# GpSimd scales the exponent half of VectorE's exponentials; the last VectorE step becomes a 16-bit integer sum

## The chip, the core and the metric

The kernel runs on one core of a Trainium2 chip. A core has five engines that work side by side and are held together by semaphores: TensorE (PE in the profile; its weight loads are PEld), VectorE (DVE), ScalarE (ACT), GpSimd (POOL) and SyncE (SP), which only issues DMAs. SBUF is the on-chip memory, PSUM the memory into which TensorE accumulates. The metric is the time of the program on the device in microseconds (us); lower is better.

## What is computed

Two layers; each is an attention block followed by a token-mixing MLP, on x of [1, 2048, 640], with the same weights in both layers.

```python
def _A_ref(x, wqkv, wo):                      # 32 heads of 20
    q, k, v = ...(x @ wqkv)                   # B,H,S,Dh each
    scores = jnp.einsum("bhqd,bhkd->bhqk", q, k) * (Dh ** -0.5)
    p = _softmax(scores, axis=-1)
    o = jnp.einsum("bhqk,bhkd->bhqd", p, v)
    return (heads side by side) @ wo
def _B_ref(x, w1, b1, w2, b2):                # mixes along the tokens
    h = _layernorm(x, axis=-1)
    u = _gelu(jnp.einsum("bsd,sf->bdf", h, w1) + b1)
    return transposed(jnp.einsum("bdf,fs->bds", u, w2) + b2)
x = A_x
x = x + _A_ref(_layernorm(x), A_wqkv, A_wo);  x = x + _B_ref(_layernorm(x), ...)
x = x + _A_ref(_layernorm(x), A_wqkv, A_wo);  x = x + _B_ref(_layernorm(x), ...)
```

What matters here is the softmax: 32 heads of 2048 by 2048 exponentials in each layer, 134 million in a layer.

## The kernel before, in words

**Tiling.** Scores are made transposed, keys on the 128 partitions, 512 queries in the free dimension, for 4 heads at a time (a group). One such 128 x 512 block of one head is called a chunk here. A layer has 4 query blocks x 8 groups x 16 key tiles = 512 units (`NU`, line 252) of 4 chunks (`NH`), 2048 chunks; the two layers have 4096. A unit's scores (lines 642 to 647) go to PSUM tiles `S` of three or two chunks; ScalarE takes the exponential of a whole `S` tile into a bf16 tile `P` (`emit_exp`, L715); TensorE multiplies `P` with the values and adds into the PSUM tile `acc` (`emit_PV`, L1268), where a column of ones gives the softmax's denominator as well.

**Exponentials on VectorE.** Some chunks are taken from ScalarE. TensorE writes such a chunk's scores to the PSUM tile `Dt` (`ve_admit`, lines 507 to 554), and VectorE makes exp of it from integer operations. The scores come scaled so that the float is a fixed-point base-2 exponent with 16 fraction bits. Two chunks form a pair `p` with slots 0 and 1:

- `first` (L544): add the exponent's bias, clamp at zero, write as int32 into `ew`; one instruction for each chunk, reading PSUM. The upper 16 bits of each word are the whole part of the exponent, the lower 16 the fraction; both are read as 16-bit elements at a step of two.
- the shift (L604): `ey` = the fraction, scaled and moved, as f16. It runs on GpSimd where `ve_shift` (lines 607 to 625) could place it, else on VectorE (`shifted`).
- `squared` (L574): `ey` = `ey` * `ey`, a dense f16 product over the pair.
- `mantissa` (L578): `et` = (`ey` + constant) * fraction, over the pair, written as f32: the mantissa's part of the result's bits.
- `expo` (L587): `Pd` = whole * 128 + `et`, over the pair, written as int16 into the bits of the bf16 tile `Pd`. `Pd` then goes to L1268 like a `P`.

**What sets the order.** The instruction streams of VectorE, ScalarE, GpSimd and TensorE are written out by a planner that runs when the kernel is built. It keeps a clock for each engine (`pem`, `dvm`, `acm`) and one for the SBUF port that VectorE and GpSimd share (`port`). Work on VectorE is a list of `Proc` objects, each a row of steps (planned cost, function, wait, and a fourth element if the step needs the shared port: `locks()`, line 294). `pump` (line 332) takes the step that can start first, by rank among those within 0.06 us: normalisation of a finished `acc` 0, evacuation of other PSUM tiles 1, `first` 2, layer norm 3, the pair's other steps 4. A locking step starts no earlier than `port["pool"]` (line 302), the planned end of GpSimd's last shift.

`ve_shift` is called from `Proc.step` (lines 306 and 307) when a step that does not lock and costs at least `POOL_HOST` = 0.45 us is about to run: that step is the **host** of a GpSimd instruction, which is issued beside it and held by a semaphore until the VectorE instruction before the host has ended (`after_vector`). Hosts are the instructions that read PSUM or have one SBUF input: L544, the transposes L752 and L776, the evacuations L364, L366, L1018, L1023, L1071 and L1105 and the statistics L828 and L831.

`ve_admit` gives VectorE another chunk whenever `Dt` is free, the planned backlog of VectorE is at most `VE_BACKLOG` = 7 us and, for a new pair, no more than two pairs are queued; so the planner keeps VectorE full, and what VectorE takes ScalarE does not have to do (`take_acts`, line 484). VectorE's pairs exist only after the first weights and keys have been made (`late`, `feed_ended`) and until the units run out. TensorE's gaps are filled with products of zeros (`zero_wave`, L704), which keep it busy and whose results are not used.

Of the kernel before, what the change touches and what calls it, by code (L numbers as in the profile page):

```python
# [12 lines left out]
BF16 = mybir.dt.bfloat16  # L13
F32 = mybir.dt.float32
I32 = mybir.dt.int32
I16 = mybir.dt.int16
# [3 lines left out]
ALU = mybir.AluOpType  # L20
# [38 lines left out]
POOL_EY = 0.58  # L59
POOL_NEXT = 0.144  # L60
POOL_TO_DVE = 0.1
POOL_LATE = 0.3
POOL_HOST = 0.45
POOL_DMA = 0.9

HOLD = 3
# [11 lines left out]
def kernel(  # L78
# [12 lines left out]
    nc = tc.nc  # L91
# [11 lines left out]
    def after_vector(inst):  # L103
        earlier = next(i for i in reversed(nc.cur_bb.bb.instructions) if i.engine == nc.vector.engine)
        tc.add_manual_dep(inst.ins, earlier.name,
                          mybir.DependencyInfo(mybir.DependencyClass.Sync, mybir.DependencyReason.DATA), reason="port")
# [113 lines left out]
    def attention(st, x_in_ap, x_mid, uacc_l, feed, feed_stack):  # L220
# [14 lines left out]
        late = {}  # L235

        def open_late():
            def pool(name, bufs):
                late[name] = p1.enter_context(tc.tile_pool(name=f"{name}{layer}", bufs=bufs, reuse_waits="tile"))
            pool("xsp", 3 if x_in_ap.dtype == F32 else 2)  # L240
            pool("w1sp", 2)
            pool("ustg", 2)
            pool("atp", NG + 4)
            pool("vew", 3)
            pool("vet", 1)
            pool("vey", 2)
            pool("vep", 3)
        T2 = ntmp.tile([128, 16, 32], BF16, name="T2")
        nc.gpsimd.memset(T2[:], 0.0)
        h2_tiles, tt_state, attnT_tiles = {}, {}, {}  # L250
# [9 lines left out]
        port = dict(pool=0.0, t=0.0)  # L260
# [25 lines left out]
        class Proc:  # L286
# [17 lines left out]
            def step(self):  # L304
                at = self.start()
                if self.eng is dvm and not self.locks() and self.steps[0][0] >= POOL_HOST:
                    ve_shift(at)
                cost, fn, wait = self.steps.popleft()[:3]
                end = at + cost
                self.eng["t"] = end - self.eng["over"]  # L310
                self.ready = end + self.eng["next"] + wait
                fn(end)
                if not self.steps:
                    self.eng["procs"].remove(self)
                    if self.after is not None:
                        self.after(end)
# [190 lines left out]
        def ve_admit(t):  # L507
            now = pem["t"] - WAVE
            if (not late or early[0] or cursor[0] >= NCH or Dbank.free > now + 0.02 or
                    backlog(now) > CFG["VE_BACKLOG"]):  # L510
                return
            p, slot = ve_state["pair"], ve_state["slot"]
            if slot == 0:
                if len(ve_procs) > 2:
                    return
                done = backlog(now) + 2 * 1.2 + 4.0 + CFG["VE_MARGIN"]
                n = max(cursor[0] // NH + max(CFG["VE_LEAST"], math.ceil(done / 1.8)), ve_state["unit"] + 1)
                if n >= NU:
                    n = max(cursor[0] // NH + math.ceil((done - CFG["VE_MARGIN"]) / 1.8), ve_state["unit"] + 1)
                if n >= NU and Dbank not in banks:  # L520
                    banks.append(Dbank)
                if n >= NU or not unit_ok(units[n], now - 0.1):
                    return
                ve_state["unit"] = n
            n = ve_state["unit"]
            js = {c[1] for c in tiles[t]}
            free = [j for j in range(NH) if (n, j) not in on_dve]
            c = (n, next((j for j in free if j not in js), free[0]))
            clash = c[1] in js
            on_dve.add(c)  # L530
            loc[c] = (p, slot)
            ve_users.setdefault(p, []).append(c)
            ve_shifted.setdefault(p, [])
            Dt = Dbank.alloc()
            s_matmul(Dt[:, :], *c)
            at = pe_wave("S", cells=0.25) if clash else now
            Dbank.free = 1e9
            if slot == 0:
                ve_w[p] = late["vew"].tile([128, 2, 512], I32, name="ew")
            w = ve_w[p]  # L540

            def first(end):
                Dbank.free = end + DVE_TO_PE
                nc.vector.tensor_scalar(out=w[:, slot, :], in0=Dt[:, :], scalar1=127.0 * FIX,  # L544
                                        scalar2=0.0, op0=ALU.add, op1=ALU.max)

            def firsted(end):
                pieces.append((p, slot, w, end))
                if slot == 1:
                    ve_enqueue(p, 2, end + DVE_NEXT)  # L550
            submit(Proc(2, [(0.69, first, 0.0)], at + PE_TO_DVE, after=firsted))
            ve_state["slot"] = 1 - slot
            if slot == 1:
                ve_state["pair"] = p + 1

        def ve_enqueue(p, k, ready):
            w = ve_w.pop(p)
            wh = w[:, 0:k, :].rearrange("p a b -> p (a b)").bitcast(I16).rearrange("p (c two) -> p c two", two=2)
            frac = wh[:, :, 0].bitcast(U16)
            whole = wh[:, :, 1]  # L560
            vet, vep = late["vet"], late["vep"]
            box = {}

            def shifted(end):
                todo = [x for x in range(k) if x not in ve_shifted[p]]
                c0, c1 = 512 * todo[0], 512 * (todo[-1] + 1)
                for x in list(pieces):
                    if x[0] == p:
                        pieces.remove(x)
                shift(nc.vector, ve_y_of(p)[:, c0:c1], frac[:, c0:c1])  # L570

            def squared(end):
                y = ve_y_of(p)[:, 0:512 * k]
                nc.vector.tensor_tensor(out=y, in0=y, in1=y, op=ALU.mult)  # L574

            def mantissa(end):
                box["t"] = vet.tile([128, 1024], F32, name="et")
                nc.vector.scalar_tensor_tensor(out=box["t"][:, 0:512 * k], in0=ve_y.pop(p)[:, 0:512 * k],  # L578
                                               scalar=MANT_C * MANT_K ** 2, in1=frac, op0=ALU.add, op1=ALU.mult)

            def expo(end):
                Pd = vep.tile([128, 2, 512], BF16, name="Pd")
                ve_P[p] = Pd
                bits = Pd[:, 0:k, :].rearrange("p a b -> p (a b)").bitcast(I16)
                ve_ready[p] = end + DVE_TO_PE
                ve_procs.popleft()
                nc.vector.scalar_tensor_tensor(out=bits, in0=whole, scalar=128.0, in1=box["t"][:, 0:512 * k],  # L587
                                               op0=ALU.mult, op1=ALU.add)
            steps = [(0.15 + 0.27 * (k - len(ve_shifted[p])), shifted, 0.0, True)] if len(ve_shifted[p]) < k else []
            steps += [(0.69, squared, 0.0, True), (1.22, mantissa, 0.0, True), (1.22, expo, 0.0, True)]  # L590
            proc = Proc(4, steps, ready, allow=lambda me: ve_procs[0] is me and (len(me.steps) > 1 or p - 3 not in ve_users))
            proc.pair, proc.ready = p, max([ready] + ve_shifted_at.get(p, []))
            ve_procs.append(proc)
            dvm["procs"].append(proc)

        ve_y, ve_shifted, ve_shifted_at = {}, {}, {}

# [6 lines left out]
            return engine.tensor_scalar(out=out_ap, in0=in_ap, scalar1=MANT_K / FIX, scalar2=-MANT_K * MANT_S,  # L604
                                        op0=ALU.mult, op1=ALU.add)

        def ve_shift(at):
            if not pieces or pieces[0][3] + POOL_NEXT > at + POOL_LATE or port["t"] > at + POOL_LATE:
                return
            if pieces[0][0] - 2 in ve_y:  # L610
                return
            p, slot, w, end = pieces.popleft()
            half = w[:, slot, :].bitcast(I16).rearrange("p (c two) -> p c two", two=2)[:, :, 0].bitcast(U16)
            inst = shift(nc.gpsimd, ve_y_of(p)[:, 512 * slot:512 * (slot + 1)], half)
            after_vector(inst)
            done = max(at + POOL_NEXT, end + POOL_NEXT, port["t"]) + POOL_EY
            port["pool"] = port["t"] = done
            ve_shifted[p].append(slot)
            ve_shifted_at.setdefault(p, []).append(done + POOL_TO_DVE)
            for proc in ve_procs:  # L620
                if proc.pair == p:
                    cost, fn, wait, lock = proc.steps.popleft()
                    if cost > 0.5:
                        proc.steps.appendleft((cost - 0.27, fn, wait, lock))
                    proc.ready = max(proc.ready, done + POOL_TO_DVE)
# [739 lines left out]
        t = 0  # L1365
# [455 lines left out]
```

## Time and profile before

| | us |
|---|---|
| median of 3 runs (1764.66 to 1764.97) | 1764.69 |
| the profiled execution: its own time | 1764.66 |
| its span, first to last instruction | 1762.8 |
| busy: PE / ACT / DVE / POOL | 1686.9 / 1676.8 / 1536.8 / 379.6 |
| granted TensorE clock | 1.0 |

The profile is of one execution. A line of its groups names a source line, the engine, the operation, what is written and read by the program's names, the shapes, the count, then the busy time, the mean of one in ns, and the idle time of that engine before them with what ended it. The windows view gives each engine's busy time, and its number of instructions, in a stretch of the span. A line of the timeline gives start, duration, the instruction, and the idle time before it.

### The profile page before, as it was taken

Reading aid. Unit: us, or ns where it says so; the run is one execution under the profiler, and the core shown is the slowest. Engines: PE = TensorE matmul, PEld = TensorE weight load, DVE = VectorE, ACT = ScalarE, POOL = GpSimd, SP = SyncE. Lnnn points to the kernel's source line nnn. Section 1 sums busy time; section 2 is a strip of 40 time slices with the busy share of each in tenths; the row PEclk is TensorE's granted clock in tenths of the full one; section 3 lists DMA queues with packets and bytes.
Section 4 is the critical chain, followed back from the end, with each engine's and each line's share of the span. In section 5 each row is a group of like instructions: output and inputs, shape, how many; then the busy total and the mean of one; then the engine's idle time right before and its main releaser. Section 6 shows DMA issues by size and latency. Waiting matters only on the chain. (4 is left out here: it accounts for less than half of the span.)

```text
span 1762.8 us, 42985 instructions
## 1 busy us (share of the span) xinstructions
PE 1686.9 (96%) x18044; PEld 669.7 (38%) x18044; DVE 1536.8 (87%) x2356; ACT 1676.8 (95%) x1510; POOL 379.6 (22%) x597
## 2 busy tenths in 40 slices
PE   9999999999999999999999999999999999999999
PEld 3333333333333344444444433333333333444455
DVE  7479999999999999999543469999999999999973
ACT  8999999999999999999779999999999999999970
POOL 2112222222232223221000011122222332322200
PEclk9999999999999999999999999999999999999999
DMA  3200000010122110123322100001001220101345
GB/s 116 39 2 1 1 2 2 16 32 2 35 63 72 38 36 14 40 76 118 113 79 74 56 20 1 1 2 39 24 2 61 68 80 14 62 2 52 102 125 178
DMA packets 103010, 81.85 MB, mean 46 GB/s; under 512 B 50976, under 2 KB 87456, under 8 KB 102816
## 3 DMA queue, kind: packets, MB, share of 16 engines
q1 hardware_dynamic: 97280, 71.22, 13.7%
q0 software_dynamic: 5536, 7.88, 1.4%
q8 instruction: 141, 2.31, 0.6%
q14 instruction: 53, 0.43, 0.1%
HBM read 55.48 MB, written 23.59 MB: 45 GB/s over the span
## 5 line engine op out<-in xcount | busy, mean ns | idle before, releaser
L715 ACT ACTIVATE P<-S 128x1024 bf16<-128x1024 f32 (+1 forms) x1442 | 1629.2, 1387 | 13.0 <-PE S L645 12.7
L645 PE MATMUL S<-QTq,KT 32*128 32x512 bf16 (+1 forms) x4488 | 577.5, 337 | 65.6 <-ACT P L715 46.7
L604 POOL TENSOR_SCALAR ey<-ew 128x512 f16<-128x512 uint16 x494 | 305.0, 617 | 1019.7 <-DVE et L578 415.9
L645 PEld LDWEIGHTS <-KT 32*128 32x128 bf16 x5136 | 232.4, 91 | 534.4 <-issue 507.0
L1268 PE MATMUL acc<-P,Vaug 128*32 128x512 bf16 (+1 forms) x4472 | 362.4, 343 | 0.3 <-ACT P L715 0.3
L544 DVE TENSOR_SCALAR ew<-Dt 128x512 int32<-128x512 f32 x496 | 338.3, 682 | 17.2 <-PE Dt L645 11.1
L704 PE MATMUL acc<-zr,zw 128*32 128x512 bf16 x4408 | 343.8, 383 | 1.2 <-POOL zr L151 1.2
L587 DVE SCALAR_TENSOR_TENSOR Pd<-ew,et 128x1024 int16<-128x1024 int16 x248 | 311.9, 1258 | 1.2
L578 DVE SCALAR_TENSOR_TENSOR et<-ey,ew 128x1024 f32<-128x1024 f16 x248 | 302.4, 1219 | 2.4
L645 PE MATMUL Dt<-QTq,KT 32*128 32x512 bf16 (+1 forms) x648 | 190.8, 332 | 0.0
L574 DVE TENSOR_TENSOR ey<-ey 128x1024 f16<-128x1024 f16 x248 | 174.2, 702 | 0.4
L1268 PEld LDWEIGHTS <-Vaug 128*32 128x32 bf16 x5120 | 103.0, 94 | 169.9 <-issue 158.9
L704 PEld LDWEIGHTS <-zw 128*32 128x32 bf16 x4620 | 116.9, 96 | 99.5 <-issue 54.7
L845 POOL TENSOR_TENSOR rstd<-veps,mhalf 128x1 f32<-128x1 f32 x60 | 49.0, 817 | 252.3 <-DVE veps L843 197.3
L1268 PE MATMUL acc<-Pd,Vaug 128*32 128x512 bf16 (+1 forms) x648 | 97.5, 334 | 0.2 <-DVE Pd L587 0.2
L1119 PE MATMUL misc<-hh,wq_pad 128*128 128x512 bf16 x300 | 87.3, 383 | 0.0
L1010 PEld LDWEIGHTS <-w1st 128*128 128x128 bf16 x672 | 52.1, 97 | 58.6 <-issue 46.5
L1119 PE MATMUL misc<-hh,wk_pad 128*128 128x512 bf16 x250 | 73.2, 383 | 0.0
L752 DVE STREAM_TRANSPOSE T<-acc 128x512 f32<-128x512 f32 (+1 forms) x81 | 56.3, 695 | 19.3 <-PE acc L1268 19.0
L1059 PE MATMUL misc<-wo_pad,attnT 128*128 128x320 bf16 x384 | 72.8, 302 | 0.3 <-DVE x1s L1071 0.2
L1010 PE MATMUL misc<-x1last,w1st 128*128 128x320 bf16 x384 | 72.1, 302 | 0.0
L364 DVE CAST KT<-misc 128x512 bf16<-128x512 f32 x50 | 34.3, 685 | 20.8 <-PE misc L1119 20.7
(143 smaller groups left out, 1083.8 us busy)
## 6 DMA issues: line engine op xcount, KB each, us to landing
w2s<-in_B_w_dram SPq DMA_DIRECT2D x16, 768.0 KB
uacc<-ustg POOLq DMA_DIRECT2D x24, 320.0 KB, 2.7
x1in<-xd SPq DMA_DIRECT2D x24, 320.0 KB
w1st<-in_B_w_dram SPq DMA_DIRECT2D x24, 256.0 KB
xd<-x2s SPq DMA_DIRECT2D x16, 320.0 KB
xin<-xd SPq DMA_DIRECT2D x16, 320.0 KB
w1st<-in_B_w_dram SPq DMA_DIRECT2D x24, 192.0 KB
xd<-x1s SPq DMA_DIRECT2D x12, 320.0 KB
```

Of the source, the lines that this page charges most:

```text
L544: nc.vector.tensor_scalar(out=w[:, slot, :], in0=Dt[:, :], scalar1=127.0 * FIX, scalar2=0.0, op0=ALU.add, op1=ALU.max)
L574: nc.vector.tensor_tensor(out=y, in0=y, in1=y, op=ALU.mult)
L578: nc.vector.scalar_tensor_tensor(out=box["t"][:, 0:512 * k], in0=ve_y.pop(p)[:, 0:512 * k], scalar=MANT_C * MANT_K ** 2, in1=frac, op0=ALU ...
L587: nc.vector.scalar_tensor_tensor(out=bits, in0=whole, scalar=128.0, in1=box["t"][:, 0:512 * k], op0=ALU.mult, op1=ALU.add)
L604: return engine.tensor_scalar(out=out_ap, in0=in_ap, scalar1=MANT_K / FIX, scalar2=-MANT_K * MANT_S, op0=ALU.mult, op1=ALU.add)
L645: pe(nc.tensor.matmul(out_ap[:, c0:c0 + w], lhsT=KT[32 * j:32 * j + 32, g, kt * 128:(kt + 1) * 128], rhs=get_QT(st, qb)[32 * j:32 * j + 32 ...
L704: pe(nc.tensor.matmul(bank[32 * j:32 * j + 32, 0:w], lhsT=zw[:], rhs=zr[:, :, 0:64].to_broadcast([128, w // 64, 64]), start=start, stop=st ...
L715: nc.scalar.activation(out=P[:, 0:ncs, :].rearrange("p a b -> p (a b)"), in_=St[:, 0:ncs, :].rearrange("p a b -> p (a b)"), func=ACT.Exp, ...
L1010: pe(nc.tensor.matmul(t[:, 0:w], lhsT=w1_of[(p, ft)][:, sti, :], rhs=rows_in[sti][:, c0:c1], start=(sti == 0), stop=(sti == n_in - 1)))
L1059: pe(nc.tensor.matmul(t[:, 0:w], lhsT=attnT[g][:, ttl * 128:(ttl + 1) * 128], rhs=wo_pad[:, g, c0:c1], start=(g == 0), stop=(g == NG - 1)))
L1119: pe(nc.tensor.matmul(t[:, :], lhsT=wpad[:, dt_, g, :], rhs=hT[:, dt_, tb * 512:(tb + 1) * 512], start=(dt_ == 0), stop=(dt_ == NDT - 1)))
L1268: pe(nc.tensor.matmul(acc[32 * j:32 * j + 32, a0:a0 + w], lhsT=Vaug[:, (kt * H + hh_) * VW:(kt * H + hh_) * VW + 32], rhs=P[:, slot, c0:c0 ...
```

## The change

`ve_base` is new. Where a host finds no shift to place, it may place a **base** instead: GpSimd multiplies the whole part of one chunk (512 elements at a step of two, int16) by 128 into that chunk's half of the result tile `Pd`, as int16. `expo` then differs by what was placed: both halves based, one dense `tensor_tensor` sum of `Pd` and `et` in place; one half based, two instructions of 512 elements, a sum for that half and the old operation for the other; none, the old instruction. `et` is int16 in place of f32, so that the sum has 16-bit operands only. `Pd` has four buffers in place of three, and is allocated by whichever of `ve_base` and `expo` comes first. The planner's cost of `expo` is 1.22, 1.03 or 0.69 us for no, one or two bases.

```diff
--- before.py
+++ after.py
@@ -61,6 +61,9 @@
 POOL_TO_DVE = 0.1
 POOL_LATE = 0.3
 POOL_HOST = 0.45
+POOL_BASE_HOST = 0.45
+VEP_BUFS = 4
+VE_ADD = (1.22, 1.03, 0.69)
 POOL_DMA = 0.9
 
 HOLD = 3
@@ -244,7 +247,7 @@
             pool("vew", 3)
             pool("vet", 1)
             pool("vey", 2)
-            pool("vep", 3)
+            pool("vep", VEP_BUFS)
         T2 = ntmp.tile([128, 16, 32], BF16, name="T2")
         nc.gpsimd.memset(T2[:], 0.0)
         h2_tiles, tt_state, attnT_tiles = {}, {}, {}
@@ -304,7 +307,7 @@
             def step(self):
                 at = self.start()
                 if self.eng is dvm and not self.locks() and self.steps[0][0] >= POOL_HOST:
-                    ve_shift(at)
+                    ve_shift(at, self.steps[0][0])
                 cost, fn, wait = self.steps.popleft()[:3]
                 end = at + cost
                 self.eng["t"] = end - self.eng["over"]
@@ -546,6 +549,7 @@
 
             def firsted(end):
                 pieces.append((p, slot, w, end))
+                bases.append((p, slot, w, end))
                 if slot == 1:
                     ve_enqueue(p, 2, end + DVE_NEXT)
             submit(Proc(2, [(0.69, first, 0.0)], at + PE_TO_DVE, after=firsted))
@@ -558,7 +562,6 @@
             wh = w[:, 0:k, :].rearrange("p a b -> p (a b)").bitcast(I16).rearrange("p (c two) -> p c two", two=2)
             frac = wh[:, :, 0].bitcast(U16)
             whole = wh[:, :, 1]
-            vet, vep = late["vet"], late["vep"]
             box = {}
 
             def shifted(end):
@@ -574,24 +577,62 @@
                 nc.vector.tensor_tensor(out=y, in0=y, in1=y, op=ALU.mult)
 
             def mantissa(end):
-                box["t"] = vet.tile([128, 1024], F32, name="et")
+                box["t"] = late["vet"].tile([128, 1024], I16, name="et")
                 nc.vector.scalar_tensor_tensor(out=box["t"][:, 0:512 * k], in0=ve_y.pop(p)[:, 0:512 * k],
                                                scalar=MANT_C * MANT_K ** 2, in1=frac, op0=ALU.add, op1=ALU.mult)
 
             def expo(end):
-                Pd = vep.tile([128, 2, 512], BF16, name="Pd")
+                Pd = ve_result(p)
                 ve_P[p] = Pd
-                bits = Pd[:, 0:k, :].rearrange("p a b -> p (a b)").bitcast(I16)
                 ve_ready[p] = end + DVE_TO_PE
                 ve_procs.popleft()
-                nc.vector.scalar_tensor_tensor(out=bits, in0=whole, scalar=128.0, in1=box["t"][:, 0:512 * k],
-                                               op0=ALU.mult, op1=ALU.add)
+                for x in [x for x in bases if x[0] == p]:
+                    bases.remove(x)
+                based = ve_based.pop(p, [])
+                parts = [range(k)] if len(based) in (0, k) else [[x] for x in range(k)]
+                for part in parts:
+                    lo, hi = 512 * part[0], 512 * (part[-1] + 1)
+                    bits = Pd[:, 0:k, :].rearrange("p a b -> p (a b)").bitcast(I16)[:, lo:hi]
+                    t = box["t"][:, lo:hi]
+                    if part[0] in based:
+                        nc.vector.tensor_tensor(out=bits, in0=bits, in1=t, op=ALU.add)
+                    else:
+                        nc.vector.scalar_tensor_tensor(out=bits, in0=whole[:, lo:hi], scalar=128.0, in1=t,
+                                                       op0=ALU.mult, op1=ALU.add)
             steps = [(0.15 + 0.27 * (k - len(ve_shifted[p])), shifted, 0.0, True)] if len(ve_shifted[p]) < k else []
-            steps += [(0.69, squared, 0.0, True), (1.22, mantissa, 0.0, True), (1.22, expo, 0.0, True)]
-            proc = Proc(4, steps, ready, allow=lambda me: ve_procs[0] is me and (len(me.steps) > 1 or p - 3 not in ve_users))
+            cost = VE_ADD[min(2, len(ve_based.get(p, [])) + 2 - k)]
+            steps += [(0.69, squared, 0.0, True), (1.22, mantissa, 0.0, True), (cost, expo, 0.0, True)]
+            proc = Proc(4, steps, ready, allow=lambda me: ve_procs[0] is me and
+                        (len(me.steps) > 1 or p in ve_results or p - VEP_BUFS not in ve_users))
             proc.pair, proc.ready = p, max([ready] + ve_shifted_at.get(p, []))
             ve_procs.append(proc)
             dvm["procs"].append(proc)
+
+        ve_results, ve_based, bases = {}, {}, deque()
+
+        def ve_result(p):
+            if p not in ve_results:
+                ve_results[p] = late["vep"].tile([128, 2, 512], BF16, name="Pd")
+            return ve_results[p]
+
+        def ve_base(at):
+            for x in bases:
+                p, slot, w, end = x
+                if end + POOL_NEXT > at + POOL_LATE or port["t"] > at + POOL_LATE:
+                    return
+                if p not in ve_results and (p - VEP_BUFS in ve_users or p - 1 not in ve_results and p > 0):
+                    return
+                bases.remove(x)
+                bits = ve_result(p)[:, slot, :].bitcast(I16)
+                whole = w[:, slot, :].bitcast(I16).rearrange("p (c two) -> p c two", two=2)[:, :, 1]
+                after_vector(nc.gpsimd.tensor_scalar(out=bits, in0=whole, scalar1=128.0, scalar2=0.0, op0=ALU.mult, op1=ALU.add))
+                port["pool"] = port["t"] = max(at + POOL_NEXT, end + POOL_NEXT, port["t"]) + POOL_EY
+                ve_based.setdefault(p, []).append(slot)
+                for proc in ve_procs:
+                    if proc.pair == p:
+                        cost, fn, wait, lock = proc.steps.pop()
+                        proc.steps.append((VE_ADD[len(ve_based[p])], fn, wait, lock))
+                return
 
         ve_y, ve_shifted, ve_shifted_at = {}, {}, {}
 
@@ -604,10 +645,11 @@
             return engine.tensor_scalar(out=out_ap, in0=in_ap, scalar1=MANT_K / FIX, scalar2=-MANT_K * MANT_S,
                                         op0=ALU.mult, op1=ALU.add)
 
-        def ve_shift(at):
-            if not pieces or pieces[0][3] + POOL_NEXT > at + POOL_LATE or port["t"] > at + POOL_LATE:
-                return
-            if pieces[0][0] - 2 in ve_y:
+        def ve_shift(at, self_cost):
+            if (not pieces or pieces[0][3] + POOL_NEXT > at + POOL_LATE or port["t"] > at + POOL_LATE or
+                    pieces[0][0] - 2 in ve_y):
+                if self_cost >= POOL_BASE_HOST:
+                    ve_base(at)
                 return
             p, slot, w, end = pieces.popleft()
             half = w[:, slot, :].bitcast(I16).rearrange("p (c two) -> p c two", two=2)[:, :, 0].bitcast(U16)
```

## The prediction

> **What bounds the kernel now.** I read the busy time by stretch first, since shares over the whole span mix stages. This is the windows view, on the two stretches from the first to the last `ew` instruction of each layer, where VectorE's pairs exist (columns: the stretch, its length, then busy time and instructions of PE, PEld, DVE, ACT, POOL):
>
> ```profile
> 109.40:811.20 701.80, 672.81 (x7694) 253.68 (x7693) 687.14 (x973) 701.50 (x622) 182.28 (x286) 1.00 0.10 30
> 1037.70:1689.70 652.00, 624.19 (x7162) 240.87 (x7160) 638.86 (x924) 652.00 (x578) 166.96 (x258) 1.00 0.12 35
> ```
>
> ACT is busy for 701.5 of 701.8 and all of 652.0 us: it sets the length of both. DVE is 98% busy (1326.0 of 1353.8 us, 27.8 idle), so it has nothing to give. PE looks as busy, but the page's L704 group, products of zeros, is 343.8 us of it. POOL is idle three quarters of the time. Next, the costliest groups (page, part 5):
>
> ```profile
> L715 ACT ACTIVATE P<-S 128x1024 bf16<-128x1024 f32 (+1 forms) x1442 | 1629.2, 1387 | 13.0 <-PE S L645 12.7
> ...
> L604 POOL TENSOR_SCALAR ey<-ew 128x512 f16<-128x512 uint16 x494 | 305.0, 617 | 1019.7 <-DVE et L578 415.9
> ...
> L544 DVE TENSOR_SCALAR ew<-Dt 128x512 int32<-128x512 f32 x496 | 338.3, 682 | 17.2 <-PE Dt L645 11.1
> ...
> L587 DVE SCALAR_TENSOR_TENSOR Pd<-ew,et 128x1024 int16<-128x1024 int16 x248 | 311.9, 1258 | 1.2
> L578 DVE SCALAR_TENSOR_TENSOR et<-ey,ew 128x1024 f32<-128x1024 f16 x248 | 302.4, 1219 | 2.4
> ...
> L574 DVE TENSOR_TENSOR ey<-ey 128x1024 f16<-128x1024 f16 x248 | 174.2, 702 | 0.4
> ```
>
> VectorE makes 496 of the 4096 chunks, ScalarE the other 3600 in 1629.2 us: 0.4526 us each. ACT waits for scores only 12.7 us in all, none of it inside the two stretches. A pair costs VectorE 2 x 0.682 + 0.702 + 1.219 + 1.258 = 4.54 us, and 248 pairs are 1127 of its 1326 us. So the way to a shorter time is more chunks on VectorE: each pair more takes 2 x 0.4526 = 0.905 us from ScalarE.
>
> **What a based pair saves.** The sum of int16 has no row in this trace. From below, L574 is the same operation on 1024 dense 2-byte elements; from above, L587 as it is. Both rows include waits for GpSimd, which I take out by the timeline: L587 instructions that start clear of a shift take 1.215, L574 0.683. I take 0.683 for the sum, the row of the same shape: a pair with both halves based saves 1.215 - 0.683 = 0.53. With one half it becomes two instructions: half of 1024 elements less is 0.267 off the sum (0.42) and 0.533 off the old one (0.68), 1.10 together, less 0.08 for the overlap of neighbours (L544 lasts 0.682, the next starts 0.605 after it): 1.02, a saving of 0.19. The Trainium skill, "VectorE: DVE Perf Modes", What auto-detection actually checks, says that a two-source op makes two results a cycle if every tensor is 16-bit with step one. By it the sum costs what L574 does, int16 or f16; by the measured rows alone it could be 1.215 (rival D).
>
> `et` as int16: L587 writes int16 and takes 1.215 clear, L578 writes f32 at 1.219, so nothing. If the type cost either way the 39 ns between their means, that is 10 us of VectorE, 2 us of time by the conversion below. `Pd`'s fourth buffer: L1268 reads a `Pd` about a microsecond after it is written while pairs come 5.5 us apart (1353.8 / 248), so three were not short either; nothing.
>
> **How many bases.** I replayed the rule over this trace. The stretches hold 1,076 instructions of the hosting kind; 494 shifts are placed first. On the remaining hosts, with a chunk whose `ew` has ended, GpSimd free within 0.3 us, `expo` not begun and buffers given in order, 319 halves find a place: 126 pairs with both and 67 with one, 255 on wide hosts (512 columns, 0.68 to 0.71 us) and 64 on narrow ones (320 columns, 0.48). An estimate: the new plan will have other hosts. Gross saving 126 x 0.53 + 67 x 0.19 = 80 us of VectorE.
>
> **What the bases cost VectorE.** A base outlasts its host, and the next two-input instruction waits for it. The timeline shows it for shifts, wide host first, then narrow (DVE, then POOL):
>
> ```profile
> 401.51 0.68 DVE L544 TENSOR_SCALAR ew<-Dt 128x512 int32<-128x512 f32 x1
> 402.11 1.25 DVE L587 SCALAR_TENSOR_TENSOR Pd<-ew,et 128x1024 int16<-128x1024 int16 x1
> ...
> 513.99 0.48 DVE L1023 COPY ustg<-misc 128x320 f32<-128x320 f32 x1
> 514.39 1.46 DVE L587 SCALAR_TENSOR_TENSOR Pd<-ew,et 128x1024 int16<-128x1024 int16 x1
> ```
>
> ```profile
> 401.68 0.62 POOL L604 TENSOR_SCALAR ey<-ew 128x512 f16<-128x512 uint16 x1 [1.88 <-DVE et L578]
> ...
> 514.16 0.62 POOL L604 TENSOR_SCALAR ey<-ew 128x512 f16<-128x512 uint16 x1 [0.31 <-DVE ew L544]
> ```
>
> The first shift ends 0.19 after L587 began, and L587 lasts 1.25; the second 0.39 after, and it lasts 1.46: the waiting time is inside the instruction. Over all such places, from the host's start to the start after the next two-input instruction, a wide host with a shift costs 0.10 more than one without (1.410 against 1.314 for L574, 1.849 against 1.742 for L587), a narrow one 0.38 (1.897 against 1.513). Hosts are followed by a two-input instruction in 52% of the free wide cases and 55% of the narrow. So 255 x 0.52 x 0.10 + 64 x 0.55 x 0.38 = 13 + 13 = 26 us. The Trainium skill, "SBUF — State Buffer", Who interferes with whom, speaks against the change: it says that a VectorE instruction with two SBUF inputs and a GpSimd instruction that reads SBUF exclude each other, whoever is first. The rows show it with 0.10 and 0.38; the new sum is itself such an instruction, so it too can be held, which the prices above cover.
>
> GpSimd's own new work is 319 x 0.617 = 197 us beside 349 in the stretches; it has room. Its base on int16 has no row; below lies the memset L1439 (4364 ns for 5120 bf16, 0.44 for 512), above L845 (0.817); I take 0.617, the row with the same input step and width. At 0.44 the waits nearly go (+26 us of VectorE); at 0.817 each wait grows by 0.20. What is queued behind a base on GpSimd is the next shift, which waits for its own host anyway, the layer norm's `rstd` (60 in all, rarely next to a host) and 24 DMA issues off the critical path. SyncE's queue is not touched.
>
> **The sum.** 80 - 26 = 54 us of VectorE's time free. A new pair costs it 4.54 - 80/248 + 26/248 = 4.32, and shortens the stretch, hence VectorE's time too, by 0.905: 54 / (4.32 + 0.905) = 10.3 pairs, 20.6 chunks, 20.6 x 0.4526 = 9.3 us off ScalarE, off the stretches, off the end. Against the profiled execution's own 1764.66 us (the median of the runs is 0.03 above it): **1755.3 us**. PE's zeros give way to whatever it must do; if ScalarE had not been the bound, nothing would have come of it.
>
> **Rivals.** 0.2% (3.5 us) is about what a measurement of this kernel can tell from no change.
>
> *A, as above*, 1747 to 1761. The lower end is every pair with both bases: 248 x 0.53 = 131, less about 40 of waits, 91 / 5.1 = 18 pairs, 16 us, and a little more if the base is short.
>
> *B, the freed time is not turned into pairs*: the planner's queue limits or the free `Dt` bind instead, or bases are few. 1761 to 1766, say 1764. For it: `ew` waits 11.1 us for `Dt` already. Against it: DVE is at 98% in stretches of very different other work, with `ew` counts of 36 to 40 per 100 us, so the limit is its own time.
>
> *C, VectorE falls behind its plan*, the one on the other side. The plan books 0.58 us for a base and a start 0.144 after the host's, so a wait of 0.12 after a wide host and 0.32 after a narrow one, and admits pairs on that account. Of 319 bases 172 (54%) have a two-input instruction behind them. If the wide ones wait like narrow ones (133 x 0.26 = 35) and the product takes 0.817 (172 x 0.20 = 34), with 2 for the narrow ones VectorE is 71 us late; 27.8 are idle time that takes it up, and 43 come out as ScalarE waiting for scores behind a late `Dt` or `Pd`: 1755 + 43 = 1798. It decides from 27.8 / 172 = 0.16 us per wait over plan. Against it: shifts on wide hosts cost 0.10 under the same bookkeeping, less than planned.
>
> *D, the integer sum runs at 1.215*: nothing is saved, while the plan has booked it: 126 x 0.53 + 67 x 0.26 = 84 us late, less 28 idle, 1755 + 56 = 1811. Then the change does not do what it says.
>
> **The numbers.** A 0.66, B 0.14, C 0.12, D 0.08. Forecast 1755.3. A and B together hold 0.80 and reach from 1747 to 1766; with C's near edge I set 1747 to 1768. Faster by over 0.2%: 0.66 (A); within 0.2%: 0.14 (B); slower: 0.20 (C and D).
>
> **What would show it.** In the changed profile: L715's total down by about 9 us, with `ew` near 516 instead of 496; a `TENSOR_TENSOR` on `Pd` of 128x1024 int16 at 0.68 to 0.75 (1.2 is D); a POOL group of some 320 int16 products at 0.617; L587's old form only on 512 or unbased pairs; ACT idle before L715 still near 13 us (tens of us more is C); DVE still 98% busy in the stretches (well under that with ACT full is B). I am wrong first of all if the number of bases is far from 320 or the wait behind one far from 0.1.

## The result, and the profile after

The changed kernel takes 1757.23 us (median of 6 runs, 1757.15 to 1757.66) against 1764.68 before: ratio 0.9958, 95% interval 0.9945 to 0.9971. It is 7.45 us faster; the forecast was 9.4 less than the median, 1755.3. The profiled execution took 1757.27, its span is 1755.5. Some executions of several kernels here took about 1.1 us more than the others of the same kernel, at a granted clock of 0.999 instead of 1.000, so differences of about 1 us between medians are not read closely. Lines have moved: L715 is now L757, L544 L547, L574 L577, L578 L581, L604 L645; L600 is the old three-operand instruction, L598 the new sum, L628 the base. The groups of the page, part 5:

```profile
L757 ACT ACTIVATE P<-S 128x1536 bf16<-128x1536 f32 (+2 forms) x1434 | 1620.8, 1374 | 13.2 <-PE S L687 12.7
...
L547 DVE TENSOR_SCALAR ew<-Dt 128x512 int32<-128x512 f32 x516 | 351.5, 681 | 19.8 <-PE Dt L687 13.6
...
L581 DVE SCALAR_TENSOR_TENSOR et<-ey,ew 128x1024 int16<-128x1024 f16 x258 | 321.4, 1246 | 2.9
L628 POOL TENSOR_SCALAR Pd<-ew 128x512 int16<-128x512 int16 x303 | 186.4, 619 | 142.3 <-DVE et L581 37.4
...
L577 DVE TENSOR_TENSOR ey<-ey 128x1024 f16<-128x1024 f16 x258 | 184.4, 715 | 0.5
```

`ew` went from 496 to 516: ten pairs, 20 chunks, have moved to VectorE, and ScalarE's exponentials take 1620.8 us instead of 1629.2. It waits for scores as little as before. The last steps of the pairs, with the shapes kept apart (groups view):

```profile
L600 DVE SCALAR_TENSOR_TENSOR Pd<-ew,et 128x1024 int16<-128x1024 int16 x75 | 95.3, 1271 | 0.3
L598 DVE TENSOR_TENSOR Pd<-Pd,et 128x1024 int16<-128x1024 int16 x120 | 89.2, 743 | 4.6 <-POOL Pd L628 2.9
...
L600 DVE SCALAR_TENSOR_TENSOR Pd<-ew,et 128x512 int16<-128x512 int16 x63 | 42.9, 681 | 0.0
...
L598 DVE TENSOR_TENSOR Pd<-Pd,et 128x512 int16<-128x512 int16 x63 | 28.0, 444 | 1.7 <-POOL Pd L628 0.9
```

303 bases, then: 120 pairs with both halves, 63 with one, 75 with none. Clear of GpSimd the full sum takes 0.682 us (70 of the 120), the half sum 0.416 (38 of the 63). The two stretches, windows view (PE, PEld, DVE, ACT, POOL; both end at the last `ew`, while the second stretch in the prediction ended at the last `expo`):

```profile
109.40:806.10 696.70, 665.32 (x7564) 254.86 (x7586) 679.41 (x1029) 696.50 (x617) 282.40 (x450) 1.00 0.10 30
1033.50:1672.00 638.50, 610.15 (x6957) 232.49 (x6977) 622.06 (x960) 638.22 (x566) 259.71 (x411) 1.00 0.12 36
```

ACT is still full; DVE is at 97%, 33.7 us idle.

**Where the time came from.** The starts and ends of the exponentials in the trace cut the execution into four parts:

| us | before | after | difference |
|---|---|---|---|
| to layer 1's last exponential | 824.20 | 819.92 | -4.28 |
| from there to layer 2's first | 36.41 | 36.54 | +0.13 |
| layer 2's exponentials | 832.04 | 828.16 | -3.88 |
| from the last one to the end | 70.18 | 70.88 | +0.70 |

Twenty chunks at 0.4526 are 9.05 us; 8.16 appear in the two attention parts, and 0.83 are given back after them.

### The profile page after: what moved, and what is told of

Its sections match the earlier page's. It is cut to its first block, busy times and chain, and to the rows that moved or that the text cites. A ratio compares the mean times of both kernels' runs of the same rounds, so it can differ in the third digit from the quotient of the medians.

```text
span 1755.5 us, 43109 instructions
## 1 busy us (share of the span) xinstructions
PE 1670.5 (95%) x17783; PEld 666.8 (38%) x17864; DVE 1521.2 (87%) x2468; ACT 1668.4 (95%) x1502; POOL 577.3 (33%) x921
## 4 chain that ended last, share of the span: by engine, by line
ACT 50%; PE 24%; issue 21%; DVE 3%; POOL 0%; DMA 0%; another core or an unknown queue 0%; SPq 0%; ACTq 0%; POOLq 0%; DVEq 0%
ACT P L757 50%; PE S L687 7%; PE acc L1310 3%; PE misc L1052 2%; PE ya L1746 2%; PE acc L746 2%; PE misc L1161 1%; PE misc L1101 1%; PE um L1733 1%; PE ya L1755 1%; DVE et L581 1%; DVE ew L547 1%; PE yb L1746 1%; PE misc L1665 0%; PE Dt L1161 0%
## 5 line engine op out<-in xcount | busy, mean ns | idle before, releaser
L757 ACT ACTIVATE P<-S 128x1536 bf16<-128x1536 f32 (+2 forms) x1434 | 1620.8, 1374 | 13.2 <-PE S L687 12.7
L645 POOL TENSOR_SCALAR ey<-ew 128x512 f16<-128x512 uint16 x515 | 318.2, 618 | 727.3 <-DVE et L581 323.4
L547 DVE TENSOR_SCALAR ew<-Dt 128x512 int32<-128x512 f32 x516 | 351.5, 681 | 19.8 <-PE Dt L687 13.6
L746 PE MATMUL acc<-zr,zw 128*32 128x512 bf16 x4232 | 325.5, 382 | 1.2 <-POOL zr L154 1.2
L581 DVE SCALAR_TENSOR_TENSOR et<-ey,ew 128x1024 int16<-128x1024 f16 x258 | 321.4, 1246 | 2.9
L628 POOL TENSOR_SCALAR Pd<-ew 128x512 int16<-128x512 int16 x303 | 186.4, 619 | 142.3 <-DVE et L581 37.4
L687 PE MATMUL Dt<-QTq,KT 32*128 32x512 bf16 (+1 forms) x672 | 198.2, 332 | 0.0
L577 DVE TENSOR_TENSOR ey<-ey 128x1024 f16<-128x1024 f16 x258 | 184.4, 715 | 0.5
L600 DVE SCALAR_TENSOR_TENSOR Pd<-ew,et 128x1024 int16<-128x1024 int16 (+1 forms) x138 | 138.2, 1002 | 0.3
L598 DVE TENSOR_TENSOR Pd<-Pd,et 128x1024 int16<-128x1024 int16 (+1 forms) x183 | 117.1, 640 | 6.3 <-POOL Pd L628 3.8
L1052 PEld LDWEIGHTS <-w1st 128*128 128x128 bf16 x672 | 52.8, 97 | 57.8 <-issue 45.2
L1052 PE MATMUL misc<-x1last,w1st 128*128 128x320 bf16 x384 | 72.9, 302 | 0.0
```

Source lines behind the costliest of these rows:

```text
L598: nc.vector.tensor_tensor(out=bits, in0=bits, in1=t, op=ALU.add)
L600: nc.vector.scalar_tensor_tensor(out=bits, in0=whole[:, lo:hi], scalar=128.0, in1=t, op0=ALU.mult, op1=ALU.add)
L628: after_vector(nc.gpsimd.tensor_scalar(out=bits, in0=whole, scalar1=128.0, scalar2=0.0, op0=ALU.mult, op1=ALU.add))
L687: pe(nc.tensor.matmul(out_ap[:, c0:c0 + w], lhsT=KT[32 * j:32 * j + 32, g, kt * 128:(kt + 1) * 128], rhs=get_QT(st, qb)[32 * j:32 * j + 32 ...
L746: pe(nc.tensor.matmul(bank[32 * j:32 * j + 32, 0:w], lhsT=zw[:], rhs=zr[:, :, 0:64].to_broadcast([128, w // 64, 64]), start=start, stop=st ...
L757: nc.scalar.activation(out=P[:, 0:ncs, :].rearrange("p a b -> p (a b)"), in_=St[:, 0:ncs, :].rearrange("p a b -> p (a b)"), func=ACT.Exp, ...
```

## The experiments

The theory: ScalarE sets the time, VectorE's freed time counts only as pairs which the plan admits, and a base is worth its saving less the wait behind it. For rivals C and D of the prediction, two kernels make VectorE late.

**No base**, all else of the change kept.

```diff
-POOL_BASE_HOST = 0.45
+POOL_BASE_HOST = 9.0
```

> The changed kernel with the threshold for bases above every host's cost: no base is placed, every pair ends with the old three-operand instruction; `et` stays int16 and `Pd` keeps four buffers. My theory: only the bases pay; 248 pairs, L600 about 1.26 us each on 248, `ew` 496, 1764.7 us (within 0.5). Rival: the int16 `et` or the fourth buffer carries part of the gain; then 1758 to 1763.

Measured: 1764.61 us, ratio 1.0 (0.999 to 1.0009). `ew` 496, the mean of L600 1258 ns and of the int16 `et` 1219, as before the change. The data type and the fourth buffer are worth nothing by themselves; the rival falls.

**The plan is not told.**

```diff
-VE_ADD = (1.22, 1.03, 0.69)
+VE_ADD = (1.22, 1.22, 1.22)
```

> The changed kernel with the planner's cost of the last step left at 1.22 us for none, one or two bases: bases are placed and save what they save, but the plan does not know it. My theory: the gain comes only through pairs that the plan admits. The plan now books the bases' waits (0.12 after a wide host) without their saving, so it admits about 5 pairs fewer than before the change: `ew` near 486, 10 chunks more for ScalarE, 1764.7 + 10 x 0.45 = 1769, with VectorE idle for 60 us more in the two stretches. Rival: VectorE's freed time shortens the program by itself (fewer late results, fewer waits): 1757 to 1760.

Measured: 1773.51 us, ratio 1.0049 (1.0034 to 1.0064), slower than with no bases at all. `ew` is 486 as expected, though 313 bases save what they save; VectorE is idle 101.7 us in the stretches instead of 33.7. A faster VectorE by itself buys nothing: the rival falls. The time is 4.5 us over my figure. In the profiled execution (1774.09) the last exponential ends 5.2 us later than before the change, of which the ten chunks are 4.5; the other 4.3 lie behind it (74.5 us to the end instead of 70.2). The windows view shows this there (behind POOL stand the granted clock as a share of TensorE's full one, the DMA share and GB/s):

```profile
1706.00:1710.00 4.00, 1.96 (x17) 0.94 (x11) 3.02 (x8) 1.98 (x3) 0.67 (x2) 0.95 0.98 292
1710.00:1714.00 4.00, 4.00 (x21) 2.03 (x20) 2.55 (x4) 2.75 (x4) 0.00 (x0) 0.62 0.90 270
```

PE had little to do in the first window (1.96 of 4 us), and in the next the granted clock is 0.62. The trace's clock record has 0.50 for 3.41 us from 1709.62, behind TensorE pauses of 1.62 and 0.37 us. Two of the four executions kept a clock of 1.000 and took 1772.8 and 1772.9, the other two 1774.1; so the lower clock is worth about 1.2 of the 4.3 us. The plan had left 19 products of the MLP (L1052) for after the attention; before the change it was 12. How much of the other 3 us they carry was not tried.

**The sum without its fast form** (rival D on the chip).

```diff
-nc.vector.tensor_tensor(out=bits, in0=bits, in1=t, op=ALU.add)
+nc.vector.scalar_tensor_tensor(out=bits, in0=bits, scalar=1.0, in1=t, op0=ALU.mult, op1=ALU.add)
```

> The changed kernel with the sum of base and `et` made by the three-operand instruction (Pd x 1.0 + et), which has no fast form here: the plan is that of the changed kernel, which books 0.69, the chip needs about 1.215 for a pair and 0.68 for a half. It is rival D of the prediction on the chip. My theory: 120 x 0.53 + 63 x 0.26 = 80 us late against some 34 us of idle time, so 46 us show as ScalarE waiting for scores: about 1803, ACT idle before P tens of us. Rival: the lateness is taken up pair by pair in the plan's margin between a result and its use: 1757 to 1765.

Measured: 1819.19 us, ratio 1.0307 (1.0292 to 1.0322). VectorE is busy 80.4 us more than in the changed kernel (1601.6 against 1521.2), as expected; the two attention parts are 62.2 us longer. Of its 33.7 us idle only 15 were used up (18.4 are left), not all: hence 16 us more than I had said. ACT now waits:

```profile
ACT P L757 <- PE S L687: 39.2, 69, 8.3
ACT P L757 <- PE Dt L687: 13.5, 32, 1.2
```

This is the waits view (total, times, longest): 12.7 us in 5 waits have become 39.2 in 69, and waits behind a `Dt` product have joined them. These are 40 of the 62 us; ScalarE's busy time is 17.2 us longer as well (1685.6 against 1668.4), which was not looked into. Beyond the 15 us of idle time, nearly all the lateness shows in the time, and the speed of the sum decides the sign of the change.

**A base that reads nothing.** It leaves out the exponent part.

```diff
-after_vector(nc.gpsimd.tensor_scalar(out=bits, in0=whole, scalar1=128.0, scalar2=0.0, op0=ALU.mult, op1=ALU.add))
+after_vector(nc.gpsimd.memset(bits, 0))
```

> The changed kernel with the base's product replaced by a memset of the same 512 elements of `Pd` by GpSimd: it leaves out the exponent part, so the probabilities are not the reference's. Same plan, same VectorE instructions; GpSimd no longer reads SBUF for a base. My theory: the waits behind a base are a conflict over reads (the Trainium skill, SBUF - State Buffer, Who interferes with whom): two-input instructions next to a base fall back to their clear times (0.68 for L577 and the sum, 1.215 for L581), about 15 to 20 us less VectorE busy time, and the time of the program stays 1757.2 within 1 us, since ScalarE's work is set by the plan. Rival: the late VectorE instructions hold ScalarE back, and the time falls by 2 us or more.

Measured: 1756.93 us, against 1757.23 for the changed kernel: as good as the same. VectorE is busy 13.3 us less (1507.9), a little under the 15 to 20 expected, and about that much more idle. The same three instructions near the end, first in the changed kernel (timeline, DVE and then POOL):

```profile
1680.37 0.48 DVE L1147 TENSOR_TENSOR x1last<-Dt,xin 128x320 f32<-128x320 f32 x1
1680.77 1.53 DVE L581 SCALAR_TENSOR_TENSOR et<-ey,ew 128x1024 int16<-128x1024 f16 x1
```

```profile
1680.61 0.62 POOL L628 TENSOR_SCALAR Pd<-ew 128x512 int16<-128x512 int16 x1 [2.39 <-DVE ey L577]
```

and then with the memset:

```profile
1679.59 0.48 DVE L1147 TENSOR_TENSOR x1last<-Dt,xin 128x320 f32<-128x320 f32 x1
1679.99 1.22 DVE L581 SCALAR_TENSOR_TENSOR et<-ey,ew 128x1024 int16<-128x1024 f16 x1
```

```profile
1679.79 0.52 POOL L628 MEMSET Pd<- 128x512 int16 x1 [2.35 <-DVE ey L577]
```

The product still runs 0.46 us after L581 has begun, and L581 takes 1.53; the memset overlaps it by 0.32, and it takes 1.22. Over all of L581 that overlap a base: 1.31 beside a product (58), 1.209 beside a memset (39), 1.215 clear. The Trainium skill, "SBUF — State Buffer", Who interferes with whom, says that a VectorE instruction with two SBUF inputs conflicts with a GpSimd instruction that reads SBUF and not with one that only writes; the runs agree with both halves. The program's time hardly moved, since the plan did not.

**Every base twice** (rival C on the chip): the product is issued a second time behind the first.

```diff
 after_vector(nc.gpsimd.tensor_scalar(out=bits, in0=whole, scalar1=128.0, ...))
+nc.gpsimd.tensor_scalar(out=bits, in0=whole, scalar1=128.0, ...)
```

> The changed kernel with every base's product issued twice in a row on GpSimd (the second writes the same values); the plan counts it once. It is rival C of the prediction on the chip: the next two-input instruction waits 0.62 us longer. My theory: 119 bases have such an instruction right behind their host, up to 170 soon after, so VectorE is 75 to 105 us late; of the changed kernel's 34 us idle about 15 can be used, as with the slow sum, so 60 to 90 us show: 1817 to 1847. Rival: the lateness is taken up in the plan's margins: under 1765.

Measured: 1861.34 us (1856.38 to 1866.31), ratio 1.0546 (1.052 to 1.0573): the right side, but above my range. In the groups:

```profile
L598 DVE TENSOR_TENSOR Pd<-Pd,et 128x1024 int16<-128x1024 int16 x120 | 92.0, 766 | 48.1 <-POOL Pd L629 47.5
```

The last number is what I had left out: the sum cannot begin before its own base is done, and VectorE stood idle 47.5 us for that. In the changed kernel this wait was 2.9. The waits inside instructions, which I had counted alone at 75 to 105 us, are smaller: VectorE is busy 44.2 us more (1565.4 against 1521.2).

**Wide hosts only**, and **bases that may start later**:

```diff
-POOL_BASE_HOST = 0.45
+POOL_BASE_HOST = 0.6
```

> The changed kernel with bases beside hosts of 0.6 us and more only, so none beside the 320-column ones. By the rows a base behind a narrow host costs 0.38 where a two-input instruction follows (about a third of the 65) and saves 0.19 to 0.34, so leaving them out should cost little: some 264 bases, 1 pair fewer, 1757.2 to 1758.6. Rival: the narrow ones' waits eat more than they save; then 1755.5 to 1756.8.

```diff
-if end + POOL_NEXT > at + POOL_LATE or port["t"] > at + POOL_LATE:
+if end + POOL_NEXT > at + 0.45 or port["t"] > at + 0.45:
```

> The changed kernel with bases allowed to start up to 0.45 us after their host instead of 0.3: some 356 bases instead of 303, the 53 more reaching further past their hosts. If a base were worth its average (55 us of VectorE for 303, 0.18 each), 53 more would give 10 us, 2 pairs, 1755.4. My theory: the later they start the more of the next two-input instruction they cover, so they save nothing: `ew` 516 again, 1756.9 to 1757.6.

Measured: 1759.02 (ratio 0.9969, 0.9957 to 0.9980) and 1759.37 (0.9966, 0.9954 to 0.9979). Both miss my figures on the slow side: by the medians they are 1.8 and 2.1 us over the changed kernel, though the intervals of the ratios overlap. With bases that may start later, three of the five executions were granted a clock of 0.999 and took 1759.4 to 1759.5, the two at 1.000 took 1758.3; the profiled one is of the three, and its clock record has one stretch of 3.41 us at 0.50, early in layer 2 (from 891.82). With 264 bases `ew` is 514, and 18 MLP products are left after layer 1's attention, where the changed kernel has 2: it is 38.6 us from the last exponential to the next layer's first, instead of 36.5. With 356 bases `ew` is 516 as with 303: the mean of L581 has gone from 1246 to 1259 ns, that of L598 from 743 to 798, so the 53 more bases gave back in waits about what they saved (VectorE is busy 1524.1 us against 1521.2); 12 products are left after layer 1.

**The exponent part for nothing.** No bases, one dense sum for every pair, booked at 0.69; it leaves out the exponent part.

```diff
-POOL_BASE_HOST = 0.45
-VE_ADD = (1.22, 1.03, 0.69)
+POOL_BASE_HOST = 9.0
+VE_ADD = (0.69, 0.69, 0.69)
...
-nc.vector.scalar_tensor_tensor(out=bits, in0=whole[:, lo:hi], scalar=128.0, in1=t, op0=ALU.mult, op1=ALU.add)
+nc.vector.tensor_tensor(out=bits, in0=t, in1=t, op=ALU.add)
```

> What the change would be worth if the exponent part came for nothing: no base on GpSimd, and every pair ends with one dense int16 sum, of `et` with itself, which leaves out the exponent part; the plan books 0.69 for it. My theory: ScalarE is the bound and VectorE's time turns into pairs at 0.53 us each: 131 us / (4.01 + 0.905) = 26 pairs, 52 chunks, 23.5 us: `ew` near 548, 1741. Rival: the pairs stop growing before that (the free `Dt`, the queue of three pairs, or TensorE binds): 1748 to 1757.

Measured: 1747.22 us, ratio 0.9899 (0.9884 to 0.9914). `ew` is 548, just as worked out, and the two attention parts are 11.95 + 10.80 = 22.75 us shorter than before the change, of 23.5 expected. So the pairs do not stop growing; but the time is 6 us over my figure, and 5.4 of it lie between the layers (41.8 us against 36.4). There (windows view):

```profile
820.00:824.00 4.00, 2.02 (x8) 0.93 (x9) 2.32 (x5) 1.33 (x2) 0.55 (x1) 0.62 1.00 306
824.00:828.00 4.00, 4.00 (x17) 1.94 (x16) 2.54 (x4) 3.17 (x4) 0.00 (x0) 0.52 0.02 7
```

and in the timeline of PE:

```profile
821.98 4.43 PE L1732 MATMUL um<-hh,KT 128*128 128x512 bf16 x16 [3.08 <-DVE KT L1059]
```

21 MLP products had been left for after the attention (6 before the change). While VectorE worked off their sums, beside a layer norm, PE idled 3.08 us, and the granted clock is 0.62 and 0.52 in these two windows; the trace's clock record has 0.50 from 820.99, 2 us into the pause, for 6.83 us. The Trainium skill, "TensorE: Matmul & The Clock Gate", Part 1, says that the array falls to half its clock after an idle window of about 3.4 us and returns after as long a busy one. The half clock agrees, and it lasted 6.83 us here and 3.41 in the blind plan. The idle time does not: a pause of 3.08 us was enough here, and there pauses of 1.62 and 0.37. This execution (1748.11) is the longest of the four, at a clock of 0.998; the other three, at 0.999, took 1746.9 to 1747.4.

**What is left over at the layer's end.** PV_LATE moves the deadline of the products with V by one tile; in the second layer's plan nothing is left over then.

```diff
-    PV_LATE=4,
+    PV_LATE=5,
```

> The changed kernel with PV_LATE 5 instead of 4, by which the plan of the second layer ends with no MLP product left over after the last exponential, where the changed kernel has 16 (and 2 after the first layer); bases and pairs as many as before (516 `ew`). My theory: part of the forecast gain was given back after the last exponential by work left over there (70.9 us from it to the end, against 70.2 before the change): 70.2 or a little less, 1756.3 us (1755.8 to 1756.7). Rival: the work left over fits under the layer end's own waits and costs nothing: 1757.2.

Measured: 1755.38 us, ratio 0.9946 (0.9933 to 0.9958). `ew` 516, 307 bases, and 69.45 us from the last exponential to the end instead of 70.88: the 16 products cost 1.4 us, twice what I had said. That this run lies on the forecast of the prediction is partly luck: its gain over the changed kernel stands at the end, and the two parts with the exponentials are as long as there (820.51 and 827.71 us, against 819.92 and 828.16). L1052 in that part, the changed kernel first (windows view for that line alone: PE busy and instructions, PEld):

```profile
1684.62:1755.50 70.88, 2.67 (x16) 1.43 (x16) 1.00 0.59 182
```

```profile
1684.75:1754.20 69.45, 0.00 (x0) 0.00 (x0) 1.00 0.60 186
```

**A faster kernel**, and the same edit on the kernel before:

```diff
-    FILL_ROOM=-0.12,
+    FILL_ROOM=-0.24,
```

> A try for a faster kernel: the changed one with FILL_ROOM -0.24 instead of -0.12, so TensorE's projections and MLP products may be placed in tighter gaps. The plan has 263 pairs (`ew` 526) and nothing left over after either layer's attention. My theory: 10 chunks less for ScalarE, 4.5 us, and 0.7 us at the end: 1752. Rival: products in tighter gaps hold up the next scores, ScalarE waits, and the time is 1757 or more.

> The kernel before the change with FILL_ROOM -0.24, to see whether what that buys belongs to the change, and the change's worth on another plan. Its plan has 253 pairs (`ew` 506). My theory: 10 chunks less than before the change, 1760 us; the change on this plan is again 10 pairs, about 8 us. Rival: 1764 or more, ScalarE waiting.

Measured: with the change 1749.10 us (ratio 0.9912, 0.9898 to 0.9925), `ew` 526 with 315 bases, nothing left over after either layer; without it 1758.87 (0.9965, 0.9951 to 0.9978), `ew` 506. So the edit is worth 6 to 8 us on either kernel and does not belong to the change, and on this plan the change is worth 9.8 us: again ten pairs, 9.05 us of ScalarE, and no gain lost at the layers' ends; the 0.7 above that was not looked into. The changed kernel with this edit beats both.

## Why the prediction was right

**The bound** held: ScalarE is full in both stretches, and its work is set by the plan. Where VectorE was made faster without the plan (the blind plan, the memset) the time did not fall.

**The price of a sum**: forecast 0.683 and 1.02 for the split pair, measured 0.682 and 0.416 + 0.681 less the overlap. Int16 runs as f16 does, as the rule of the Trainium skill, "VectorE: DVE Perf Modes", What auto-detection actually checks, had it; by the other bound it would have been D, which cost 62 us on the chip where I had said 84 - 28 = 56.

**The number of bases**: 319 forecast (126 pairs with both, 67 with one), 303 found (120 and 63). Gross 120 x 0.53 + 63 x 0.19 = 76 us instead of 80. The 1,076 hosting instructions are too many: the host lines named in the kernel's description start 939 times in the two stretches before the change, and 1,076 is near the 1,085 that do not need the port, short ones included. A `Pd` is also read later than was said: taken in order, its reads begin 3.8 us (median) after it is written, not one; three buffers were enough even so, as the no-base run shows.

**The waits**: forecast 26 us. By the groups, the last step fell from 1258 ns a pair to (95.3 + 42.9 + 89.2 + 28.0) / 258 = 990: 69 us over 258 pairs. Of that `et` takes back 27 ns x 258 = 7.0, `ey` 13 ns x 258 = 3.4, the scaling L810 62 x 38 ns = 2.4 and the idle time before the sum 6.3: 50 us net. Against the gross 76 the waits are 26, as forecast. That the totals meet is partly luck: the forecast had only the two-input instruction behind a host in it (13 + 13), while the 6.3 of idle time before the sum, 3.8 of it for the sum's own base, had no term there.

**The pairs**: 10.3 forecast, 10 found, and 26 against 26 with the exponent part for nothing. The blind plan's 486 follows by the same rule. The forecast worked them out from the chip's rows, but it is the plan's own prices that set them: with the memset VectorE had 13.3 us more to spare, and `ew` stayed 516. The two agree because the plan books nearly what the chip takes, 0.12 and 0.32 us of wait behind a wide and a narrow host where the rows had 0.10 and 0.38.

**From pairs to time** is the mis-sized term. "20.6 chunks, 20.6 x 0.4526 = 9.3 us off ScalarE, off the stretches, off the end" took all of it to the end, which got 7.4. 0.3 is the rounding of pairs; 0.83 came back after the exponentials, 0.70 of it at the end, where four more MLP products stand (16 against 12); the run with none left there ended 1.85 us earlier. The other runs bear this out, with these products counted in each trace: from the last exponential to the end it is 69.4 to 69.5 us with none or one left, 70.2 with 12 and 70.9 with 16, and between the layers 36.4 us with none, 37.3 with 12, 38.6 with 18 and 41.8 with 21 and the lower clock. The other 0.9 is in the two-chunk exponentials: the mean distance from the start of one to the next exponential rose from 0.9247 to 0.9267 us in layer 1 and from 0.9260 to 0.9279 in layer 2, 2 ns on some 600, which covers it. Why was not tried; with PV_LATE 5 it is 0.9252 in layer 2, so it changes by as much from one plan to another.

**The rivals.** B did not come about: the pairs kept growing to 274 when more VectorE time was free. C is real as a mechanism, and it was priced too low for a long base: I counted the next two-input instruction only, and the sum's wait for its own base is larger (47.5 us with doubled bases, beside 44.2 inside instructions). With bases of 0.62 us it does not decide.

## What to carry to other kernels

When a planner shares work between engines, time freed on one counts only when the plan is told of it, and then in whole units of work: divide it by the cost of a unit plus what the shorter stretch takes away. An instruction moved to GpSimd costs VectorE a wait whenever a two-input instruction stands next to it; take that wait from rows of the same kind before counting the gain. And look at what a shorter stretch leaves over at its end: here that cost 0.8 of 9 us, and 5.4 in the run that left 21 products there and let TensorE idle for 3 us.

## What the runs showed of the hardware

- A GpSimd product on 512 int16 elements at a step of two takes 619 ns, as the uint16 to f16 one does (618). Two of them back to back take 764 and 870 on average, as if GpSimd then waited for VectorE in its turn; that was not tried by itself.
- A three-operand instruction on dense int16 takes 1.28 us for 1024 elements on average where the two-operand sum takes 0.743 with the same neighbours; clear of GpSimd it is 1.215 against 0.682. Its operands being 16-bit does not help it.
- After TensorE pauses of 3.08 us (the exponent part for nothing) and of 1.62 and 0.37 us (the blind plan) the granted clock was 0.50 for 6.83 and 3.41 us. One such stretch of 3.41 us cost this program about 1.2 us: 1772.9 us without it and 1774.1 with it in the blind plan, 1758.3 and 1759.4 with bases that may start later.
